# Moving half of the turned probabilities with on-chip copies instead of DMA transfers

## Chip, cores and metric

The kernel runs on one core of a Trainium2 chip. The metric is device time in microseconds for one execution; three runs of the kernel before gave 533.55 us as median (532.98 to 538.45).

## What is computed

Decayed causal attention over 8 batches, 8 heads, 576 positions and head width 64, followed by a gated projection. In float32:

```python
scores = q @ k.T / 8                                # per batch and head, 576 x 576
decay = cum[:, None] - cum[None, :]                 # cum = cumsum(log(clip(f)))
scores = where(causal, -1e9, scores + decay)
attn = softmax(scores)                              # with + 1e-9 in the denominator
x = concat_heads(attn @ v)                          # batch x 576 x 512
gate = sigmoid(sum(conv_w[k] * shifted(x, k) for k in range(5)))
out = (gate * (x @ w_val)) @ w_out
```

## The kernel before, in words

The unit of work is a pair of heads: 8 batches with 4 pairs each give 32 pairs, numbered i. For a pair, 128 partitions hold either two heads of 64 channels, or 128 query rows. The queries of a head are four blocks of 128 rows plus a first piece of 64 rows that both heads share a tile for. Block t sees EXT[t] = 192, 320, 448 or 576 keys.

The steps of a pair, with their lines:

- Scores, `plan_s`: TensorE adds a decay product (`st`, `pkr` or `pl`) and the product of q and k (`Xr`) into PSUM banks, in four groups (the groups with 576, 448, 320+192 and 64 keys).
- Row minimum, L451 on VectorE (DVE): it scales and masks the scores in PSUM and leaves `negm`. A short second instruction reads the accumulator out.
- Exponential, L455 on ScalarE (ACT): PSUM to the tiles P (Pa, Pb for both heads, Pl for the first piece), with the row sum in `zs`. After it the PSUM bank is free for other products.
- Turning, `plan_pt`, L492 and L497 on DVE: 32x32 blocks are transposed from P into T, which has 2 x 1568 columns (CW = 1568). T is double (r = i % 2). The last one, L497, takes Pl, after Pl has been scaled by POOL at L474.
- Moving, L498 to L502: a transposed 32x32 block is still in the partitions of its rows; the product with v needs its keys in 64 partitions of their half. So eight transfers a pair, issued by SyncE (SP), carry 32 partitions x 1568 columns (196 KB) each from T to U, one for each row quarter n and each column half c. U is double too (r = i % 2), so the moves of pair i wait for the product of pair i - 2.
- Product with v, `plan_pv`: 108 matmuls `banks<-U,vt` of 64x64 quadrants, all of one pair in a row.
- The normalised result goes to x32 (L548 and the copies of L554, which show as L275), is split into a rounded high part xh and a low part xl, and the gate convolution is made of multiplications (L282, ACT L280) and additions (L591). Every four pairs, `plan_moe` makes the projection by w_val (`banks<-xh,wall` and `xl`), multiplies by the gate, and projects by w_out (`banks<-wall,hh` and `hl`).

At the start the two weight matrices are decoded from integers into a high and a low part by DVE, ACT and POOL (L678 to L715).

What sets the order: every step is a node of `Plan` with an engine (or several that may do it, `any_`) and keys that it reads and writes. The order of all nodes, and the engine of each `any_` node, is not computed when the kernel is built: it is a packed table, `ORDER`, which `Plan.order` unpacks. Each engine runs its instructions in that order; an instruction at the head of an engine's queue that waits holds all that is behind it. SP issues nearly all transfers, in one queue. Helper functions record the instruction, so all matmuls show as L260, all copies and casts as L275 and all transfers as L287.

Of the kernel before, what the change touches and what calls it, by code (L numbers as in the profile page):

```python
# [14 lines left out]
P = 128  # L15
D = 64
# [30 lines left out]
    "nzHzabvOeNMWhkch&sg22q~fmv4+@0yg__GTt(bOG$5J~P$Uld8MXvo1p{yfoCrt3dGP1RdE^!3GBS;7MRXuGzyN>&UL$7^3kWijgIqxlAcv865DyWzkp{RO"
    "zJVM?Od@uoYEeAE1W19$$Z@0wXvWw99}od{10MK6R0;s0m?$2~gtDU^pr4|-$o;@!0F5G`q$o8i3~xk5P%WrY{3PCo`i#~f?a0=wjw}=MC?G`=G51m1kTUoP"
    "3X7(o&!EnuUZUQjyvR{t@~bcuhJks8UPLdUTYxBX8a;<Tjd_pygxZO$LEb>!MOn~pG#_&S*$#AJx`1w=8^cD6&|gq6^eVa!@MRAGgTN)!HIx`rg{i?rFe%J^"
    "z=82%PNL;#J$eE)i_&0>m|rlBm`7Rlm;uaRnE9;NS!5E2G!HCes<CxgC>DnmVij02mV=!F&Sv#w^=6G{O=S&a-Of6STn1JE9oC9n1lBN{m^+w<m>6~k)`OnG"  # L50
    "FW{H6hO;(+2)YVggAQe<vp;4@vt8IAmYI#tPN7eu0SF1A&fb;H%VtAFkc}*GwkdlQGl`kOEMN%Pj%++(U-m^pefF=}gV_hs53-+Tzt8@ZEhR7sC`c#z6@CN1"
    "jK4w{AT*-Y1Pz2oFcH9n6+D`70sSlXHbDY$K)etWBm$Ypp3SbN)KRc_3jP4L5o;r~V_#;!&F;iDV{c(=2?q&{gl2+|kcJ%3K9#)>k|un~hT+2mHeQ6^MfjU^"
    "pCHHU@xAEdj8lv*!cI~<p&Q$W9U%;1&t#v^t|c{+4w6(PG45XiK>SEDQa4B{Tmz&DGC`On2uTW(iDW1FNMX_=>~ri3>~`WFBAX~8ns8}S6{H!`Oaha8AnlMb"
    "ES5+ic0pbe-V)kLy^#IH!^8o|Ammc^wd^O5MeI9lfEXuQh;HIXEFMS4@o^hi0C$!&PMRXwaTr_=X@E3LdQ9pi-6k3E5xfuYz{`nx;(Nj;!g1m$;%VXpWEL_6"
    "N#PqPO_T}NEDKGZgAmDn@;s@VxJZhS`-xpdKW-JW2)RXBhO9#XXd9jY?IWI`prIk0joMD>qzqFYQ+(7ON-yO&`4l;c8>b9VrYQ52Fmo3^Os&H0#a$v_BeTgO"
    "@&ocy@&VjgTqEuRt`FCYV?ht$kKrfCv*eTbpYhjmw{ZRVT6_=w73Bu`E_pk74|zZNF!>DmJlR5aljUSR`31QT&!qCG%ajcYnEDfrog>Owp`fV*>M%}2ea3i<"
    "`<?h3evWvCah@Tirm0obCGvjiVd^4di80N%NbRG}F@DEApgyI3p~7e{S#Mbv7=w%<MjxY}@r1Za{)6~8@h{>CBgw2{)-czJtBmKk7r58BLE;(edFp%WC+cV1"
    "X9l0CVM>@r=08MG7QiGj7s(7Jis@t0*=(AK_8#{Mhow<y4(3bhTWT+Rf;vmRLA^`8PdvnIWd6o%Wp*%8S>!BE);bwXdB@_jhnYH-l?7$tSY#H5b)0&NdY!Fd"
    "8`*>G)tn*x5F22xvQTUYX`O|pe0>mXZk9Mpoh4z9GAEgytWZ`e%fa@ruQG2kSrh?9O3_f>Fh4Ns*+<!CijyLyMc66!Ip$@ikfmU)F*lhr%mro@yN11=dzjn8"
    "Zev$x)n#?D4LKw19`-nUhP}XsaEvrB%|Y{0G_-v*N6y}yFl`%cH|-EDO7Z5{Sdkn{mOCqzQ=fA*2hG_o+#~#)BjhMJ4V)%UOHNx(n1v!ac~v>`9DR<CW94+^"  # L60
    "T*&dU`f{GpMsmh-j?vPr{+u=TCcBl>!Fj{}z>aZtaH?3(X+Z9D&Rh;E_ayBiZ7`>rQ^y&~nWru0kaC&1WDbYp;siO-+~pi$t|AvnzePL7YNOqwjnH1x{-&jK"
    "8*-a+&*fguJ<Y9Qb#c47eOx@9Nl#Jkar?O+X;*V^=8ka3xGH)V?HAgOyt{eLECYR-JIK}LT5~=05WO|GBiBKn<1TVNyw9{W{b$xLdOr=IM|eE?Ppn^9@3;UD"
# [724 lines left out]
```

## Time and profile before

| what | value |
|---|---|
| median of three runs | 533.55 us (532.98 to 538.45) |
| the profiled execution's own time | 533.03 us |
| its span, first to last instruction | 531.3 us |
| mean granted TensorE clock | 0.974 |
| busy: PE, DVE, ACT, POOL | 482.3, 418.2, 309.4, 263.6 us |

The span is what the profile covers; 1.7 us lie outside it. Busy time is the time in which an engine ran instructions; idle time before an instruction is put down to what released it. "PE" is TensorE's matmul part, PEld its weight loads, SPq the queue of SyncE that issues transfers.

### The profile page before, as it was taken

What the parts mean: (1) busy time and instruction counts of PE and PEld (TensorE: products, weight loads), DVE (VectorE), ACT (ScalarE), POOL (GpSimd) and SP (SyncE); (2) the same over time, 40 slices, a digit from 0 to 9 for tenths busy, and PEclk for the clock granted to TensorE, in tenths of its full rate; (3) what the DMA queues carried; (4) which work ended last, traced back from release to release, by engine and by line L of the source; (5) the groups of instructions that cost most, each with busy time, mean ns of one, the idle gap of its engine ahead of it and who ended that gap; (6) DMA issues with size and microseconds to landing.
All of it is one profiled execution on the core that took longest, in us unless ns stands there. A gap on an engine that the chain in (4) does not pass through costs nothing.

```text
span 531.3 us, 15167 instructions
## 1 busy us (share of the span) xinstructions
PE 482.3 (91%) x5816; PEld 396.6 (75%) x5816; DVE 418.2 (79%) x1132; ACT 309.4 (58%) x869; POOL 263.6 (50%) x301
## 2 busy tenths in 40 slices
PE   6549798989899999998999979999999999999996
PEld 5347576868678877787787868778787876889885
DVE  4978988879888887786998849789887787788731
ACT  3546556546666665586586546566666576574420
POOL 4102412136748653776445836754757576664510
PEclk9769979999999999999999989999999999999999
DMA  7498789895789999789889899878999997977112
GB/s 294 154 238 236 203 223 241 230 273 170 198 221 246 218 223 270 199 259 264 211 211 260 217 227 223 234 231 217 267 200 245 241 251 199 239 181 190 54 49 80
DMA packets 50265, 114.04 MB, mean 215 GB/s; under 512 B 11664, under 2 KB 28048, under 8 KB 50192
## 3 DMA queue, kind: packets, MB, share of 16 engines
q1 hardware_dynamic: 50144, 112.99, 81.1%
q8 instruction: 46, 0.75, 0.7%
q14 instruction: 27, 0.22, 0.2%
q10 hardware_dynamic: 48, 0.07, 0.0%
HBM read 51.70 MB, written 9.96 MB: 116 GB/s over the span
## 4 chain that ended last, share of the span: by engine, by line
PE 54%; DVE 20%; DMA 8%; ACT 7%; issue 4%; POOL 3%; SPq 2%; DVEq 0%; ACTq 0%; POOLq 0%
PE banks L260 53%; DVE banks L451 7%; ACT P L455 6%; DVE T L492 5%; DMA U<-T 4%; SPq L287 2%; DMA zb<-zd 1%; DVE negm L451 1%; DMA zd<-zt 1%; PE banks L363 1%; DMA ot<-in_w_out_dram 1%; DMA Xr<-in_x_dram 1%; POOL gate L591 1%; DVE x L548 1%; DVE gate L680 1%
## 5 line engine op out<-in xcount | busy, mean ns | idle before, releaser
L455 ACT ACTIVATE P<-banks,negm 128x192 f32<-128x192 f32 (+3 forms) x256 | 146.6, 578 | 95.1 <-DVE negm L451 90.6
L451 DVE CUSTOM_DVE_ANT_0 banks<-banks,mk 128x192 f32<-128x192 f32 (+3 forms) x256 | 138.0, 574 | 34.9 <-PE banks L260 23.6
L591 POOL TENSOR_TENSOR gate<-gate,tm 128x576 f32<-128x576 f32 x85 | 121.5, 1432 | 40.6 <-ACT tm L280 12.5
L492 DVE STREAM_TRANSPOSE T<-P 128x384 f32<-128x384 f32 (+3 forms) x128 | 121.4, 963 | 24.7 <-ACT P L455 13.0
L260 PE MATMUL banks<-Xr 64*128 64x288 f32 (+4 forms) x704 | 119.9, 417 | 1.1 <-issue 0.9
L260 PE MATMUL banks<-U,vt 64*64 64x128 f32 (+1 forms) x3456 | 103.0, 264 | 16.3 <-DMA U<-T 13.9
L260 PEld LDWEIGHTS banks<-U,vt 64*64 64x64 f32 x3456 | 97.6, 140 | 25.8 <-issue 9.1
L260 PE MATMUL banks<-xh,wall 128*128 128x288 f32 x512 | 111.8, 301 | 2.3 <-ACT P L455 1.1
L260 PE MATMUL banks<-wall,hh 128*128 128x512 f32 x288 | 92.9, 404 | 2.9 <-ACT P L455 1.3
L260 PEld LDWEIGHTS banks<-xh,wall 128*128 128x128 f32 x512 | 84.4, 188 | 12.2 <-issue 4.9
L260 PEld LDWEIGHTS banks<-Xr 64*128 64x128 f32 (+1 forms) x704 | 72.0, 190 | 10.9 <-issue 2.1
L260 PE MATMUL banks<-xl,wall 128*128 128x288 f32 x256 | 75.5, 295 | 0.0
L260 PE MATMUL banks<-st,pkr 64*128 64x288 f32 (+3 forms) x320 | 61.1, 398 | 15.2 <-ACT P L455 8.0
L260 PEld LDWEIGHTS banks<-wall,hh 128*128 128x128 f32 x288 | 51.3, 188 | 19.7 <-issue 4.1
L260 PEld LDWEIGHTS banks<-st,pkr 64*128 64x128 f32 x320 | 31.9, 187 | 37.7 <-ACT P L455 10.9
L260 PE MATMUL banks<-wall,hl 128*128 128x512 f32 x144 | 56.4, 391 | 0.0
L282 POOL TENSOR_SCALAR tm<-x,cw 128x576 f32<-128x576 f32 x48 | 37.7, 786 | 27.2 <-DVE gate L591 24.8
L455 ACT ACTIVATION_READ_ACCUMULATOR P<-banks,negm 128x1 f32 x256 | 50.6, 198 | 0.0
L260 PEld LDWEIGHTS banks<-xl,wall 128*128 128x128 f32 x256 | 48.1, 188 | 0.4
L280 ACT ACTIVATE tm<-x,cw 128x576 f32<-128x576 f32 x50 | 38.5, 775 | 7.0 <-DVE gate L591 6.4
L451 DVE DVE_READ_ACCUMULATOR2_ANT negm<- 128x1 f32 x288 | 40.0, 139 | 0.1
L560 POOL TENSOR_TENSOR xl<-x,xh 128x576 fp32r<-128x576 f32 x22 | 31.9, 1454 | 15.5 <-ACT xh L275 12.1
(94 smaller groups left out, 487.7 us busy)
## 6 DMA issues: line engine op xcount, KB each, us to landing
U<-T SPq DMA_DIRECT2D x256, 196.0 KB, 5.6
Xr<-in_x_dram SPq DMA_DIRECT2D x32, 608.0 KB, 7.0
...
```

The source lines that it names most:

```text
L260: nc.tensor.matmul(out, lhsT=lhsT, rhs=rhs, start=start, stop=stop)
L280: eng.activation(out=out, in_=in_, func=AF.Copy, scale=col)
L282: eng.tensor_scalar(out=out, in0=in_, scalar1=col, scalar2=0.0, op0=ALU.mult, op1=ALU.add)
L287: lambda e: (nc.sync if e == "SP" else nc.scalar).dma_start(out=out, in_=in_), reads, writes, **kw)
L363: nc.tensor.transpose(out=bank(wk)[:, n * P:(n + 1) * P], in_=ident, identity=ident)
L451: nc.vector.tensor_tensor_reduce(out=sl, in0=sl, in1=add, op0=ALU.add, op1=ALU.min, scale=-0.125, scalar=3.0e38, accum_out=negm[r][:, col])
L455: nc.scalar.activation(out=dst, in_=bank(key)[:, a0:a0 + ext], func=AF.Exp, bias=negm[r][:, col], scale=-1.0, accum_out=zs[r][:, col])
L492: dve("DT", dt(2 * w), base + 0.35 + 0.03 * n, lambda t=t, w=w: nc.vector.transpose(out=blocks(64 * FB[t], [(32, 2), (64, 2 * t + 3), (CW, ...
L548: nc.vector.tensor_tensor(out=bass.AP(to.tensor, to.offset, [to.ap[0], (P, 4), (32, 2), (1, 32)]), in0=bank(keys[n])[:, 0:L0 // 2].rearran ...
L560: any_("xl", {"POOL": 1.4, "DVE": 0.67}, p, lambda eng: eng.tensor_tensor(out=xl[s], in0=xv, in1=xh[s][:, :].bitcast(F32), op=ALU.subtract ...
L591: any_("cva", {"POOL": 1.5, "DVE": 0.66}, pp, lambda eng, to=to: eng.tensor_tensor(out=gt, in0=gt, in1=to, op=ALU.add), [tk, gk], [gk])
L680: dve(cls, one, p, lambda: nc.vector.tensor_scalar(out=m, in0=hw, scalar1=0x1FF, scalar2=None, op0=ALU.bitwise_and), uk + kg, kh)
```

## The change

In `plan_pt` of the kernel before, eight transfers a pair move T to U. Of these, the four with c = n % 2 have the same 32 partitions as source and as destination. In the changed kernel two copies a pair (one for each e) write all 128 partitions of U[:, e] from the column half e of T; in two of the four row quarters of each the copied data is what is wanted. The other four transfers stay and overwrite the other two quarters, so each of them is ordered behind the copy of its e. A copy may run on ACT, DVE or POOL, as the order table says.

```diff
     def load_pair(i):
         r = i % XB
-        load("load", 1.55, i - (1.0 if i else 9.0), Xr[r], x[i], (), [("Xr", r)], early=i == 0)
+        load("load", 1.62, i - (1.0 if i else 9.0), Xr[r], x[i], (), [("Xr", r)], early=i == 0)
...
         dve("DT", 0.16, base + 0.5, lambda: nc.vector.transpose(out=blocks(LO, [(CW, 2)]), in_=Pl[r]), [("Pl",)], [("T", r, 4)])
+        for e in range(2):
+            any_("UC", {"ACT": CW / 1200.0 + 0.06, "DVE": CW / 1920.0 + 0.15, "POOL": CW / 1450.0 + 0.25}, base + 0.53 + 0.01 * e, lambda eng, e=e: copy(
+                eng, U[r][:, e], Tt[:, CW * e:CW * e + CW]), [("T", r, k) for k in range(5)], [("U", r, n, c) for n in (e, e + 2) for c in range(2)])
         for n in range(4):
-            for c in range(2):
+            for c in (1 - n % 2,):
                 a = D * (n // 2) + 32 * c
-                load("U", 0.87, base + 0.55 + 0.01 * n, U[r][a:a + 32, n % 2], Tt[32 * n:32 * n + 32, CW * c:CW * c + CW],
+                load("U", 0.93, base + 0.55 + 0.01 * n, U[r][a:a + 32, n % 2], Tt[32 * n:32 * n + 32, CW * c:CW * c + CW],
                      [("T", r, k) for k in range(5)], [("U", r, n, c)], hold=0.63)
```

The whole table `ORDER` is replaced as well:

```diff
 ORDER = (
-    "c-l=;2}soG|DO5Ied*ly=$tyYbLyNrr_QN!I!6U%25AXp24x9p2I(fGTaZ?eZb7;Q<rbtBlo_O}kgh_y3FQ`~Tad0nx(WZ9+<t$)@O`i6^SsaVd|n;M3W9=g"
+    "c-mc52}o9X_kQ2|?)$zkzWcuK`@Zj+kXDdZkXDdZkj?~Y4Wu(cIt6JHnA1So1ZfSV6_gdEQ;<$UIt6JHq&1K>L0SX<Qop{BKbL#&x#xGzbDnda!wrKjfgXZx"
...
```

The matmuls are the same in number and shape. Counted over the whole program, other instructions change engine with the table:

| instructions | ACT | DVE | POOL | SP |
|---|---|---|---|---|
| copy U<-T 128x1568 (new) | 0 to 35 | 0 to 1 | 0 to 28 | |
| transfer U<-T 32x1568 | | | | 256 to 128 |
| multiplication tm<-x,cw 128x576 | 50 to 63 | 14 to 10 | 48 to 39 | |
| multiplication gate<-x,cw 128x576 | 11 to 19 | 3 to 2 | 14 to 7 | |
| addition gate<-gate,tm 128x576 | | 27 to 37 | 85 to 75 | |
| eviction ot<-banks 128x512 | 27 to 30 | 9 to 6 | | |
| cast wall<-gate 128x512 | 4 to 7 | 4 to 1 | | |
| copy x<-banks 64x64 | 46 to 40 | 18 to 24 | | |

The first place is SP's queue at the moves of pair 0 (T_83 and U_85 are the tiles of even pairs, zd and zb the sums on their way to all partitions and back). Before:

```order
L287 DMA gate<-in_w_val_dram 128x1024
L287 DMA zd_67<-zt_96 128x32
L287 DMA U_85<-T_83 32x1568 x4
L287 DMA zb_98<-zd_67 64x4x128 x2
L287 DMA U_85<-T_83 32x1568 x4
```

Now:

```order
L283 DMA gate<-in_w_val_dram 128x1024
L283 DMA zd_67<-zt_96 128x32
L283 DMA U_85<-T_83 32x1568
L283 DMA zb_98<-zd_67 64x4x128
L283 DMA U_85<-T_83 32x1568
L283 DMA zb_98<-zd_67 64x4x128
L283 DMA U_85<-T_83 32x1568 x2
```

Four transfers of U stand where eight stood; the first of them waits for a copy on POOL and the second for one on ACT, and the two transfers of zb are still among them.

The second place is ACT's queue at the exponentials of pair 13 (negm_91 and zs_93 are the tiles of odd pairs; xh_107 belongs to pair 11). Before:

```order
L455 ACTIVATE P_81,zs_93<-banks,negm_91 128x448
L280 ACTIVATE gate<-x_100,cw 128x576
L455 ACTIVATE P_80,zs_93<-banks,negm_91 128x576 x2
L455 ACTIVATE P_81,zs_93<-banks,negm_91 128x448
L275 COPY x_101<-banks 64x64
L595 ACTIVATE gate<-gate 128x576
L455 ACTIVATE Pl_82,zs_93<-banks,negm_91 128x64
L275 CAST xh_107<-x_101 128x576
L455 ACTIVATE P_80,zs_93<-banks,negm_91 128x320
```

Now:

```order
L451 ACTIVATE P_80,zs_93<-banks,negm_91 128x576
L271 COPY U_85<-T_83 128x1568
L276 ACTIVATE tm<-x_100,cw 128x576 x2
L594 ACTIVATE gate<-gate 128x576
L451 ACTIVATE P_80,zs_93<-banks,negm_91 128x320
L271 COPY x_101<-banks 64x64 x2
L271 CAST xh_107<-x_101 128x576
L451 ACTIVATE P_80,zs_93<-banks,negm_91 128x320
L451 ACTIVATE P_81,zs_93<-banks,negm_91 128x192 x2
L451 ACTIVATE Pl_82,zs_93<-banks,negm_91 128x64
```

Between the last of the long exponentials (576 and 448 columns) and the first of the short ones (320, 192, 64) there now stand a copy of pair 12 and two multiplications beside the gate's activation; before, only a small copy and the gate's activation stood there ahead of the first short one.

## Rows read from the trace of the kernel before

**Rows 1.** Page, part 1: busy us (share of the span) and instructions.

```profile
PE 482.3 (91%) x5816; PEld 396.6 (75%) x5816; DVE 418.2 (79%) x1132; ACT 309.4 (58%) x869; POOL 263.6 (50%) x301
```

**Rows 2.** Windows, PE alone: stretch, its length, busy us, granted clock, DMA share, GB/s.

```profile
0.00:100.00 100.00, 75.28 (x759) 0.88 0.79 224
100.00:200.00 100.00, 92.12 (x1219) 1.00 0.91 226
...
400.00:500.00 100.00, 98.47 (x1328) 1.00 0.82 208
```

**Rows 3.** Waits of PE: what it waited for, us in total, times, longest.

```profile
PE banks L260 <- DMA U<-T: 13.9, 5, 5.0
PE banks L260 <- ACT P L455: 13.4, 19, 2.6
...
PE banks L260 <- ACT Pl L455: 3.4, 2, 2.8
```

**Rows 4.** Timeline, pair 0 from the last transpose to its product with v.

```profile
23.60 0.23 DVE L497 STREAM_TRANSPOSE T<-Pl 128x64 f32<-128x64 f32 x1
...
26.48 1.75 SPq L287 DMA_DIRECT2D zb<-zd  x2
28.28 2.52 SPq L287 DMA_DIRECT2D U<-T  x4
...
32.85 0.69 PE L260 MATMUL banks<-U,vt 64*64 64x128 f32 x4 [5.01 <-DMA U<-T]
...
35.45 4.81 PE L260 MATMUL banks<-U,vt 64*64 64x128 f32 x98 [1.90 <-DMA U<-T]
```

**Rows 5.** Timeline, four later products with v; in brackets the idle time before.

```profile
50.13 2.98 PE L260 MATMUL banks<-U,vt 64*64 64x128 f32 x108
...
113.04 1.69 PE L260 MATMUL banks<-U,vt 64*64 64x128 f32 x56 [1.74 <-DMA U<-T]
...
251.83 3.35 PE L260 MATMUL banks<-U,vt 64*64 64x128 f32 x108 [1.38 <-DMA U<-T]
...
310.04 4.74 PE L260 MATMUL banks<-U,vt 64*64 64x128 f32 x108 [3.88 <-DMA U<-T]
```

**Rows 6.** Page, parts 3 and 6: the queue's packets; issues, KB each, us to landing.

```profile
q1 hardware_dynamic: 50144, 112.99, 81.1%
...
U<-T SPq DMA_DIRECT2D x256, 196.0 KB, 5.6
```

**Rows 7.** Windows, all engines: busy us of PE, PEld, DVE, ACT, POOL, then PEclk, DMA, GB/s.

```profile
27.00:40.00 13.00, 6.08 (x110) 5.26 (x110) 9.82 (x28) 5.85 (x18) 0.56 (x2) 0.63 0.91 235
306.00:320.00 14.00, 10.12 (x141) 8.63 (x141) 7.47 (x20) 6.17 (x22) 4.17 (x7) 0.88 0.93 225
```

**Rows 8.** Groups by shape: busy us, mean ns of one, and idle us before them.

```profile
L282 POOL TENSOR_SCALAR tm<-x,cw 128x576 f32<-128x576 f32 x48 | 37.7, 786 | 27.2 <-DVE gate L591 24.8 <-DVE x L548 0.6
...
L275 ACT CAST xh<-x 128x576 fp32r<-128x576 f32 x30 | 20.1, 670 | 13.7 <-DVE x L548 12.9 <-DVE x L275 0.6
...
L474 POOL TENSOR_SCALAR Pl<-Pl,zr 128x64 f32<-128x64 f32 x32 | 11.0, 343 | 51.4 <-DVE zr L465 45.1 <-ACT ot L662 4.1 <-PE banks L260 2.2
...
L275 ACT CAST pl<-pk 64x64 fp32r<-64x64 f32 x28 | 6.7, 240 | 7.6 <-PE banks L260 7.4
```

**Rows 9.** Groups by shape, ACT: a multiplication, and the exponentials of 320 and 192 columns.

```profile
L280 ACT ACTIVATE tm<-x,cw 128x576 f32<-128x576 f32 x50 | 38.5, 775 | 7.0 <-DVE gate L591 6.4 <-POOL gate L591 0.4
...
L455 ACT ACTIVATE P<-banks,negm 128x320 f32<-128x320 f32 x64 | 33.3, 524 | 29.2 <-DVE negm L451 28.5 <-DVE T L492 0.4
...
L455 ACT ACTIVATE P<-banks,negm 128x192 f32<-128x192 f32 x64 | 26.6, 418 | 31.1 <-DVE negm L451 30.2 <-DVE gate L688 0.5
```

**Rows 10.** Timeline: a DVE instruction beside a POOL one, and the same shape later.

```profile
22.14 1.26 POOL L568 TENSOR_TENSOR tm<-ident,cw 128x640 f32<-128x640 f32 x1
...
22.32 1.36 DVE L680 TENSOR_SCALAR gate<-ot 128x512 int32<-128x512 int32 x1
...
31.39 0.43 DVE L680 TENSOR_SCALAR gate<-gate 128x512 int32<-128x512 int32 x1
```

More of the change, by code (lines that the diff above doesn't have):

```diff
@@ L47 @@
[L47 to L62, printed above, removed]
@@ new lines @@
+    "R(K!uJXC_zB16z5v;-}I=b*LV8t69gZg3a02|NXD1=mB{puNy(=r9xl{|I^qY6p)&=b<A|4?GIL4!#Q>he8l)*b+1WH^Dl=J7FGJ6t)6A0B?rX!@q%*;9cN0"
+    "STA@G`~&PHECZ{CU5DL;)xf*q{a_@b0p0`O1lta4hd0AJ;Qeqi;xc#~JO`c!{|fsJ_7m(E*m?LAcm~WxOVLYUFhB)(z!ZEMJ_jFz55q^`D_{(;1fPeG!&wLs"
+    "LI|wD@4=>F^RO$p8#onW4mJg|AiRiOz<yvWq7l)8Z~=Reoyaa^5NJgPkhRD<<RUDE+>0n8k#G|H3gQOhBeD$%LM@_IfC)$eC15Mih(x1$ku?Ab)dI8wod6Tw"
+    "4fFsX5q-#Wh>M65h%<-^Vl!d_If)!Z4k06mEMf*ZioAuKMIJ#MLuk-e^i4!RFa!wUlZZRO17HEkL5WZsQ4@$IWIbvxssZ(g@Qk2ASy6L{8N@u|C)6(}2RejK"
@@ new lines @@
+    "qD$x+^dN8z*nw_Gcc4MYW^@Z0g{(*afI5l#2<t`@k*Cn#qP{~-0`CwDz#=dMu#j`W3h)6vj2=Uep!?BNXaMp(o&o_dOQ-?#IC>5}jb1?iiuw(eK~<wXs3__x"
+    "Y6>-mLSe>H(<lmtjVWUu;%0Ct$Sm#-?g4HAw}`97Y{l%vfbeMi2NVg<#tZSs@dLyaoC<HigV9Jd7b1n2AWDb}5`rWl5{wq}59wc$1>?n>z?{MC!yLpM!5qUh"
+    ";+ycb_&U4`UxEbjz4%(lEb1)&9Ofb>g)ibs=vMq&LOWhS+zGjWAI77JBw_@U#azOy5WvLO_$B;n%s$9L2!!wv{~Dztx`=-f{w7?<-^Ck=Y+{g@B5DX$!c+W9"
+    "`~+qc(+25<+`>#^rZJa@qr?KyLx>VOiCx4-;wJ`-SqEt%VhJ=tEwPpO0>dRp32!l-kOH<FauzZ{9)$E0hatBiZNxg_E#mLQWlS%Th~0n<kn6Gc@sIJf<T`SS"
@@ new lines @@
+    "JVnHih-4L+O(v7Xq$0VIJOa57c?>a<pAugZg=805fi+;6SP|BR1!1Ql91;q<1PNl7Ay6`o>>))-bC3nd9`YdhA-R*>MeZd7P&BlaoW{;m&yuNB9(9P^M&>}r"
+    "$TQ?w@+g@E-GSYMZN(-Cjf734?W8T#1@aPEO{pimA-*S;2sMPmgeF2O^%D_B%8;r_8j_V{qJ$|1>JHMkl<z2?$S}$#%63W{wUOFHO;KIc^Vn8GC)G{qB<-T?"
+    "r*J7!N*nfjY=%-z2~vyHTIySBJ86ZArO+tHKmT4@NZ%8FB%CH3r~XW6CP}DT>O*WV^(=LQI!PU+-l7gthp11mbJ!W`0O1mL6pN;v!uDh5sAO82=HW)UT(*>b"
+    "3p+x%O!ytkWQv$dritlfCYbfi24;y_qHUywm`5qyltD@jvza-`{DF3oR!4h<y-j$FUBQBJT$+^DOX;VaB|TxzG3S|Gq@QTN(00-G)6lpB%ywo6bC@~8>}Pf}"
@@ new lines @@
+    "zomUg>tRkX9k>8)fH}roWZ$A(AYCS1BaM-UDC2~2(h_rpX=d$Ux3fFg&FmI-66au-*dcb3?V&|!L>v<*#A#?&S`GV8(rJ>5m1JF`XxLVEH+zaSPI*C^reK*g"
+    "CX|I^RdAbe_3ZPsQ|utCpFO}HrhQ-ooH6zYZHoN|<uzrPJw}_L%~9S_M%dHr1@<_5j(rq&9M_A};H<bUI25PC+RUPGCTV}t_OTAKj<Algwy}1zBrGlKD7Ty2"
+    "&)vW!@tV18&Mb|};<0w%=1E8C^R#7354WDXiNBryj#lP0<7znudJA`e+rVw-4s-X=A=Cu@03AjDNCW6~oOXJF-oRn<P*h{pRqhyfoIAyx<5K7x`aG8_l8TPg"
+    "r@6iKvvddj1m_G##8dJl94+Sv=NM;+yUfjStGTuG5WS8rq656+EG2y>9nBkJo#R~OL^xT_KF&eTAgiC%%QEp?yaW7p{_m`A{v_)>{{nrMHO%keU!r>?QOOv;"
@@ new lines @@
+    "hu_b?N<W9Yh}+9+<ykmh&OQ1=dW4tdAsJ)z5&k%TivK5TiM7CTRE4TOvf6kZyczlk>n;5WpIo)XpW_2nv-H>W4|IS*WUv|Y{A3lXN>n9es2HrOW&S%+xk^<9"
+    "W?$k=a&B=ZIHR0-PHh#2{bSWO-frFr-Wi@lR1(#QLZYN-hp1iDA!-)2h&C{Kt8TM?uDZi}z&ppg$om%e9d4ki!rRQd!n?t%7a15DkyYei1R33;ZB@IgcJcS~"
+    "H_5ikW;lzS45OOysOni2z};7Mu<DfPgJ?<wh*9Ex(SYbq)q|>!oH5arsvA{Ds*Y7ni-tuQ?uckX^jFp2RpTPE_#tnW#}?1<Bx0?23!{NSmX^gYI3(_zXo0uL"
+    "L-8|`YROSazhpqNL9&l=kip?n`1O(oNw=g&BH|um9A&7vU5vL?wPL1pr?^=X5og6Mk~*=F{}baE28VCttNFu{cF9%Am}E+Fo<U+;#9r|c@iFnYitiK;8J8Gl"
@@ new lines @@
+    "`M4y^U#S8MNCLEgC76>eN#-Tfl4XgDFOn*yfD|ni3zm6isY`l5c20azJi=&~DFr9QXT(PCUMYm%A?ud)$j-~gWW%x%S*vuP_@MX+V_eoRo082kE{W6puwX(w"
+    "D(;Y)1rcdhIwsyG-7R&<C&f=>OEN$nl9T0!rE@a3ASHMxcp{h+EX%G6Q1WT<3-L|Cyi6od%2{%iyezMk7X?LSt>BcRUokJP6YP@hmklU>lrM>U<v+{sNFPY="
+    "DdrTziV?-UVyED^U_vl2I3PGDy(rzL*{ylQc+aRvH%m`Q&q%LGZ%8*NrxeqQLxN7hn4-u(CFmE_D=)|!l-uOH<pY9;(k8*8bV>0+u_ORX9KtK|8}cK%W4eIw"
+    "vVbU@kuFHdN~Z8H`QP#*@?-LS@`G}dQltcwP9;m3QeM)alpn<yNlK_xhLn4ibJ9baR^<o5WhF>>&T!E{l1yks!cpa@=8^oF{EqyAd|AqoKx9HmuclM8PjgUn"
@@ new lines @@
+    "hw*^%gW{yZsVxXM2q!fd8CrNtGov}HIiftKR0++(F3q53TnSa-RDUV|R+41(!hp6$e@m&7Gzy!AZ{>hOC`)P4ilX+pW<_&A$kr}sgj%!~tX<S_WNO(t<wYe~"
+    "u_9M1{!#v`e58D)Bxy}rqwJ8dL)a%&Y5R0R8B1|Oc}7{Qb;;_rr?p1KF71Bppl(PvsyiV(BfO=1sB<gQvKd{!c0qSScSbj>o6s%lR&?iuM#+%yf|jT<sn{x&"
+    "O02jpyeqt}y{jG4zR|wd-q$|X3RO-ONRQS()xOlS^(4JYZ`5zm3-yiqCcR4^)ZY_66owUPMN0pTv0ic0FfA<U-x|WIZ}c;UAG9a6MOjhtt@b<ZTh#~EB~`or"
+    "n*NUIfoZ~!R&7+w8deOG2C#8Vk2aEwS5>D}eX6o*qw0w5m~E$G!N4{G>L2tc_2c?Uy}(#&tTU>NMx)CZG;USxRK3x^*Qbn!j89b0Rh`Bz<DhCmHKxKEXoe5k"
@@ new lines @@
+    "W@FLVYy3(7i~cX+-@>Q*m-<h7n4#bJtMNDEpT-_@o2p6CXlzo=8Rw1fjBFiQM>MO<Y_rge(zU97)&HjdWQ3WXn-)w)^P*|R1UA1FPN)E#P-oPA5Nb?Tlgs?b"
+    "^vu*}9yAY`zgH!7Q!14XZAPgnYNo+t5E)bku*hj}>OwlETA)^`yHr6#z+7vtGq;-C%#CKQNou-pd~7^nJ7a4y8`KW<MqOFARhKds&3n}692Xtk=8!t6?lg~@"
+    "$IK6H*Nu0LeKxF#X1ZdyVfbjiZ+>i^u`Sp}Z4J5_`>buRE^WYyXre*e0d>22gL;elmhFz~feWyd)MW$4!nH^(TkJ!&MO%%bQN3cDusKY%rdDUj^wj*){Kov="
+    "+@bza4YHFgNt4SSw3kdOyV1VY@QtC-j<)YK+*F@Zv+aFql09V?+M5kc_EvkHsnOJKzv(z^DA}7#6OKv8fcl#Ktz*V9>p(ll?Dy1@>O)SFGh?Z?tT@2VD~=lu"
@@ L105 @@
+    "D~~GAD#+@^%BKpfnpn-MmQ-u2!5}CI0Rnx#5g_<y8~oV@K#<QD@Yw_Ye8E?3(C0JA=P$(i8FbYL2f<dKUl72b?Jo#lEXZo!muTR#_sch89r;V-mz*z8*k}J2"
+    "-xoCaYRp<5XccJ<2fkhjv|bakUgHZcblrxmR|VFYfmgXgzMijf`I7y`T8n_M)&i~LL00j;^a1-?VXb%AY7c8OfUnj7uQFa^u+|%BHD(P9zFudo5BPcvXcZZ;"
+    "IwQ!}IYU=_{?DACs}Zo(>@^J#>pa(H3|-HMud{`%b_iZQgM6LVni}x0ll@Y8O*!yaq&0njuegv^E^A)MDlT}n7UF+20Il}F_6GfrwWb4TH4?Or1zAS}RyqGy"
+    "BiJh9T7|VeK&(y+v98bBX036C{|{?my=&O|9M^jKuU2cy{AW`j>wAS*R~z^`@&D+L_<x%LTGa?x-M_UxhJM}8FM0n5#lizW"
 )
```

66 lines of the change are left out of this document (21 added, 45 removed).

## The prediction, made before the changed kernel ran

> **What bounds the kernel now.** I read the busy shares first, then TensorE by stretches, then what it waits for, then the timeline at those waits. TensorE is busy 482.3 of 531.3 us [rows 1]: matmuls of unchanged number and shape fill 91% of the span, so the change can touch only the 49 us in which it is idle, and the clock at which it runs after an idle stretch. The first 100 us hold 24.7 us of that idle time (75.28 busy), the next 100 hold 7.9, and from 400 to 500 only 1.5 is left [rows 2]. By cause [rows 3]: 13.9 us for moved probabilities (U<-T), 13.4 and 3.4 us for exponentials, which free the PSUM banks for the next scores; most of the rest is the start, before any product can run, and the change leaves that. The five stalls on U are 5.01 and 1.90 us in pair 0 [rows 4], then 1.74, 1.38 and 3.88 us [rows 5], together 13.91.
>
> A stall on U costs more than its length. In the stretch from 306 to 320 us, around the one of 3.88 us, the granted clock is 0.88, and around pair 0's stalls it is 0.63 [rows 7]. The product with v after the 3.88 us stall took 4.74 us where an undisturbed one takes 2.98 [rows 5], 1.8 us more. So the stalls that this change aims at are worth 15.7 us, plus the slow product of pair 0.
>
> **What the change removes.** 128 of 256 transfers of 196 KB: 25.7 MB of 113 MB on the one queue that carries nearly everything, which keeps the 16 DMA engines busy 81.1% of the span [rows 6]. If their time goes by bytes, that falls to about 63%, an estimate. SP issues four transfers of U in 2.52 us [rows 4], 0.63 each; four fewer save 2.5 us in each chain from T to U.
>
> **Pair 0, worked out.** Before: the last transpose ends at 23.83 (23.60 + 0.23), the eight issues and the two of zb between them end at 30.80 (28.28 + 2.52), and the last wait for U ends at 35.45, 4.65 us later [rows 4]. Now a copy comes first. POOL: 343 ns for 64 columns and 786 ns for 576 [rows 8] make 0.865 ns a column and 1.64 us for 1568. ACT: 240 and 670 ns [rows 8] make 0.84 ns a column and 1.50 us. So the first issue can start at 25.5; four of U (2.52) and two of zb (about 1.4, their rows take 1.75 for two with a wait in it [rows 4]) end at 29.4, and U is there at 34.0. That is 1.4 us earlier: pair 0's stalls go from 6.9 to 5.5. The clock there stays low, since TensorE still idles for five microseconds.
>
> **The later stalls.** There I expect the three to go, 7.0 us, and the 1.8 us of slow product with the last: a U transfer lands in a median of 5.6 us [rows 6] on a queue with a DMA share of 0.8 to 0.9 [rows 2], and both the issue (2.5 us shorter) and the landing shorten, against 1.5 to 1.64 us for a copy. Sum of the removed part: 1.4 + 7.0 + 1.8 = 10.2 us. Bounds: nothing at all, if the copies start late; all 13.9 + 1.8 and, with pair 0's first product back to 2.98, some 2 us more, 18.
>
> **What it adds on ACT.** 35 copies at 1.50 are 52.5 us; 13 + 8 multiplications at 775 ns [rows 9] are 16.3; the smaller shifts (evictions and casts against copies of x) are few, and I leave them at 1. ACT goes from 309 to about 380 us, 72% of the span. What hides it is ACT's idle time ahead of the short exponentials: in the order DVE makes two transposes between the minima of the long and of the short groups, and ACT waits for `negm` 28.5 and 30.2 us there [rows 9], 1.83 us a pair. In pair 13's queue the copy stands exactly in this gap, as most ACT copies do. One copy (1.50) fits; the mean addition is 70 / 32 = 2.2 us a pair, so the cover is used up, and a pair with both copies on ACT (3.0) overruns it by 1.2. The copy adds a wait too: it needs DVE's last transpose of its pair (L497) and the product with v two pairs earlier, waits that only SP bore before. Behind it on ACT are multiplications and the four short exponentials; those release banks, and TensorE's next scores wait for them. TensorE waits 16.8 us for exponentials today [rows 3]; scaled by ACT's load, 380 / 309 = 1.23, that is +3.9, and I take +4. Bounds: 0, if the idle time hides all, to 26, if half of 35 copies pass on their 1.5 us.
>
> **What it adds on POOL and DVE.** 28 copies at 1.64 are 46 us, and POOL gives up 16 multiplications at 786 ns [rows 8], 12.6 us, and 10 additions: net less than 33 us on an engine busy 50% [rows 1]. Copies on POOL wait for T ahead of additions to the gate, which few wait for at once. DVE's ten additions more and its four to five multiplications, casts and evictions fewer leave it level. A DVE instruction beside a POOL one took 1.36 us where the same shape took 0.43 later [rows 10], 0.9 more. Should each of the 28 copies hold one DVE instruction that long, DVE loses 26 us spread over 32 pairs; TensorE sees DVE through the 16.8 us of waits for exponentials and little else, so I take +1, with bounds of 0 and 26. The Trainium skill, SBUF — State Buffer, section "Who interferes with whom", says that DVE and GpSimd share one pair of ports as an exclusive lock, for copies, casts and tensor_scalar forms and for two inputs in SBUF, and that the later one blocks for a whole instruction. The row agrees in direction. By the rule a copy could hold DVE for its full 1.64 us, 46 us in all, but DVE's minima (from PSUM) would go untouched; so I keep the term at +1.
>
> **The order chosen anew.** Matmul groups come in nearly the same sequence in the first three pairs and differ afterwards. I see no systematic gain or loss and put it at 0, with bounds of 5 us either way, the middle between the 1.5 and the 7.9 us of idle time that a stretch of 100 us has [rows 2].
>
> **Sum.** -10.2 + 4 + 1 = -5.2 us on the profiled execution's 533.03, which lies 0.5 below the median of 533.55: 527.8 us.
>
> **Rivals.**
> 1. All that waits on transfers goes. Besides the 10.2 us, pair 0's other 5.5 and its slow product go because the first moves start earlier, and ACT's gaps hide the copies: 533.0 - 18 = 515. For it: the queue is the busiest shared thing after TensorE. Against it: pair 0's chain is mostly landing time. Chance 0.20.
> 2. The gain is given back. Transfers now start only when an in-order engine reaches the copy, so U is as late as before or ACT's waits take the place of the transfers' waits: about 10 us won, 10 lost, 533. For it: SP, which used to bear the wait for T, had nothing urgent behind it, ACT has. Chance 0.20.
> 3. Slower: ACT becomes the second bound. Every copy that is not hidden pushes the short exponentials of the next pair back by 1.5 us, banks come free later, TensorE idles and then runs at a low clock. It decides from the point where 7 of the 35 copies pass on their whole length (10.5 us against 10.2 won). With one in three, 12 x 1.5 = 18, it is 533 - 10 + 18 = 541. For it: the cover of 1.83 us a pair against 2.2 added. Against it: ACT is idle 222 us today and the copies can slide. Chance 0.17.
>
> My forecast holds 0.43; its own range is 521 to 533: from 12 us won with ACT's term at 0, to 5 won and 5 paid.
>
> **How the numbers follow.** A measurement of this kernel tells about 1% from no change; the border of faster lies at 528.2. Just over half of the forecast's 0.43 falls below it, with all of rival 1: 0.45. Same takes the rest of the forecast and nearly all of rival 2: 0.35. Rival 3 and the edges: 0.20. The range reaches down to rival 1 and up to rival 3, 514 to 541, and leaves out what lies beyond both.
>
> **What would show it.** Right: TensorE's waits for U fall from 13.9 to about 5.5 us, nearly all in pair 0, whose last wait ends about 1.4 us earlier; the DMA queue's share falls towards 63% and U's median landing below 5 us; the product with v takes 2.98 us everywhere after 60 us; copies take 1.5 us on ACT and 1.6 on POOL; TensorE's waits for exponentials rise from 16.8 to about 21 us. Wrong: TensorE's busy time moves by more than 3 us; waits for U reappear at other pairs because the copy was late; ACT's copies show long waits for the product two pairs back; or TensorE's idle time behind exponentials grows by over 10 us.

## The result, and the profile after

The changed kernel takes 517.25 us (median of four runs, 516.40 to 519.22), beside 536.0 us for the kernel before on the same chip: a ratio of 0.965 (95% interval 0.957 to 0.973). That is inside the range of 514 to 541, and three times the gain of the central forecast: the profiled execution takes 517.02 us against 533.03, 16.0 less, where 5.2 were forecast. Lines of the changed kernel have numbers some four lower: L256 is L260 of before, L271 is L275, L451 is L455, L493 is L497.

Busy time by engine, from the page, against [rows 1]:

```profile
PE 477.6 (93%) x5816; PEld 393.0 (76%) x5816; DVE 423.5 (82%) x1135; ACT 371.5 (72%) x924; POOL 284.5 (55%) x307
```

The span fell from 531.3 to 515.2, by 16.1 us: 4.7 of it are busy time of TensorE (482.3 to 477.6), 11.4 its idle time (49.0 to 37.6). By stretches, against [rows 2] (busy us, granted clock, DMA share, GB/s):

```profile
0.00:100.00 100.00, 77.92 (x780) 0.90 0.63 187
100.00:200.00 100.00, 97.02 (x1322) 1.00 0.65 185
...
400.00:500.00 100.00, 97.23 (x1146) 1.00 0.48 141
```

The largest step is in the second stretch, 92.12 to 97.02 at the same clock. The DMA share is lower everywhere. What TensorE waits for, against [rows 3]:

```profile
PE banks L256 <- ACT P L451: 16.0, 16, 4.7
PE banks L256 <- DMA U<-T: 5.5, 2, 4.4
...
PE banks L359 <- POOL ident L304: 1.4, 1, 1.4
...
PE banks L256 <- ACT Pl L451: 1.2, 2, 0.7
```

The waits for U went from 13.9 to 5.5 us, those for exponentials (P and Pl) only from 16.8 to 17.2. The wait for `ident`, at the start, was longer in the kernel before:

```profile
PE banks L363 <- POOL ident L308: 5.1, 1, 5.1
```

Pair 0 on the timeline, against [rows 4]:

```profile
23.76 0.20 DVE L493 STREAM_TRANSPOSE T<-Pl 128x64 f32<-128x64 f32 x1
24.03 1.49 POOL L271 COPY U<-T 128x1568 f32<-128x1568 f32 x1 [0.58 <-DVE T L493]
24.05 1.48 ACT L271 COPY U<-T 128x1568 f32<-128x1568 f32 x1
25.54 0.61 SPq L283 DMA_DIRECT2D U<-T  x1
...
28.30 1.26 SPq L283 DMA_DIRECT2D U<-T  x2
...
32.85 0.69 PE L256 MATMUL banks<-U,vt 64*64 64x128 f32 x4 [4.35 <-DMA U<-T]
...
33.83 5.24 PE L256 MATMUL banks<-U,vt 64*64 64x128 f32 x104 [0.29 <-ACT P L451]
```

Each transfer stands behind its copy. The product goes on at 33.83 where it went on at 35.45, 1.6 us earlier; its first part starts at 32.85 as before. The last wait that the profile puts down to U ends at 32.85; the 0.29 us before 33.83 it puts down to an exponential. Later products with v, against [rows 5]:

```profile
51.05 2.83 PE L256 MATMUL banks<-U,vt 64*64 64x128 f32 x104 [1.12 <-DMA U<-T]
64.19 2.98 PE L256 MATMUL banks<-U,vt 64*64 64x128 f32 x108
...
295.08 2.98 PE L256 MATMUL banks<-U,vt 64*64 64x128 f32 x108 [0.19 <-DMA out_dram<-ot]
```

The 1.12 us in pair 1 are new: the kernel before had no stall there. After them no product waits for U again. Counted in order, the one that stood at 310.04, with a stall of 3.88 us and 4.74 us of work, is pair 18's; it now stands at 295.08 and takes 2.98. The queue and the landing of U, against [rows 6]:

```profile
q1 hardware_dynamic: 44000, 87.29, 59.2%
...
U<-T SPq DMA_DIRECT2D x128, 196.0 KB, 3.9
```

The copies, and the two short exponentials, as groups (busy, mean ns | idle time before them), the exponentials against [rows 9]:

```profile
L271 ACT COPY U<-T 128x1568 f32<-128x1568 f32 x35 | 52.1, 1504 | 3.1 <-DVE T L493 2.8 <-DMA out_dram<-ot 0.3
L271 POOL COPY U<-T 128x1568 f32<-128x1568 f32 x28 | 42.7, 1535 | 12.0 <-DVE T L493 9.7 <-DMA zb<-zd 1.3 <-issue 1.0
...
L451 ACT ACTIVATE P<-banks,negm 128x320 f32<-128x320 f32 x64 | 33.5, 525 | 20.7 <-DVE negm L447 19.0 <-DVE T L488 1.1
...
L451 ACT ACTIVATE P<-banks,negm 128x192 f32<-128x192 f32 x64 | 26.6, 417 | 15.3 <-DVE negm L447 14.7 <-DVE T L488 0.4
```

ACT reaches its copies late enough that it waits only 2.8 us for the transposes, and the idle time ahead of the exponentials has shrunk from 60.3 to 36.0 us: at most 24.3 us of the 52.1 stand where ACT used to wait for `negm`, since other instructions of ACT moved too.

### The profile page after: what moved, and what is told of

It reads as the page before. It is cut to its first block, busy times and chain, and to the rows that moved or that the text cites. A ratio compares the mean times of both kernels' runs of the same rounds, so it can differ in the third digit from the quotient of the medians.

```text
span 515.2 us, 15149 instructions
## 1 busy us (share of the span) xinstructions
PE 477.6 (93%) x5816; PEld 393.0 (76%) x5816; DVE 423.5 (82%) x1135; ACT 371.5 (72%) x924; POOL 284.5 (55%) x307
## 3 DMA queue, kind: packets, MB, share of 16 engines
q1 hardware_dynamic: 44000, 87.29, 59.2%
## 4 chain that ended last, share of the span: by engine, by line
PE 53%; DVE 25%; ACT 9%; DMA 5%; issue 4%; POOL 1%; SPq 1%; DVEq 0%; ACTq 0%; POOLq 0%
PE banks L256 53%; DVE banks L447 7%; DVE T L488 6%; ACT P L451 5%; DMA U<-T 2%; DVE x L547 2%; DMA zd<-zt 2%; DVE negm L447 1%; DVE h L620 1%; DVE gate L681 1%; ACT tm L276 1%; DMA cwu<-in_conv_w_dram 1%; SPq L283 1%; DVE gate L590 1%; DVE gate L687 1%
## 5 line engine op out<-in xcount | busy, mean ns | idle before, releaser
L451 ACT ACTIVATE P<-banks,negm 128x576 f32<-128x576 f32 (+3 forms) x256 | 146.4, 578 | 55.6 <-DVE negm L447 51.1
L447 DVE CUSTOM_DVE_ANT_0 banks<-banks,mk 128x320 f32<-128x320 f32 (+3 forms) x256 | 137.9, 575 | 30.9 <-PE banks L256 15.9
L488 DVE STREAM_TRANSPOSE T<-P 128x640 f32<-128x640 f32 (+3 forms) x128 | 121.1, 963 | 12.8 <-ACT P L451 10.9
L590 POOL TENSOR_TENSOR gate<-gate,tm 128x576 f32<-128x576 f32 x75 | 107.9, 1441 | 36.1 <-DVE gate L590 13.0
L256 PE MATMUL banks<-Xr 64*128 64x288 f32 (+4 forms) x704 | 118.3, 418 | 0.5 <-DMA Xr<-in_x_dram 0.5
L256 PE MATMUL banks<-xh,wall 128*128 128x288 f32 x512 | 111.4, 301 | 2.3 <-ACT P L451 2.2
L256 PEld LDWEIGHTS banks<-U,vt 64*64 64x64 f32 x3456 | 93.7, 136 | 16.7 <-issue 11.2
L256 PE MATMUL banks<-U,vt 64*64 64x128 f32 (+1 forms) x3456 | 98.9, 258 | 7.4 <-DMA U<-T 5.5
L256 PE MATMUL banks<-wall,hh 128*128 128x512 f32 x288 | 92.8, 403 | 1.3 <-ACT ot L661 0.7
L256 PEld LDWEIGHTS banks<-xh,wall 128*128 128x128 f32 x512 | 84.1, 188 | 11.0 <-issue 5.3
L256 PE MATMUL banks<-st,pkr 64*128 64x288 f32 (+3 forms) x320 | 61.7, 401 | 19.4 <-ACT P L451 12.8
L256 PEld LDWEIGHTS banks<-Xr 64*128 64x128 f32 (+1 forms) x704 | 71.8, 191 | 9.5 <-DMA Xr<-in_x_dram 0.7
L256 PE MATMUL banks<-xl,wall 128*128 128x288 f32 x256 | 75.4, 295 | 0.0
L256 PEld LDWEIGHTS banks<-wall,hh 128*128 128x128 f32 x288 | 51.3, 188 | 19.3 <-issue 6.8
L256 PEld LDWEIGHTS banks<-st,pkr 64*128 64x128 f32 x320 | 31.3, 189 | 42.0 <-ACT P L451 16.0
L256 PE MATMUL banks<-wall,hl 128*128 128x512 f32 x144 | 56.3, 391 | 0.0
L271 ACT COPY U<-T 128x1568 f32<-128x1568 f32 x35 | 52.1, 1504 | 3.1 <-DVE T L493 2.8
L276 ACT ACTIVATE tm<-x,cw 128x576 f32<-128x576 f32 x63 | 47.9, 774 | 8.7 <-DVE gate L590 6.4
L451 ACT ACTIVATION_READ_ACCUMULATOR P<-banks,negm 128x1 f32 x256 | 50.8, 199 | 0.0
L271 POOL COPY U<-T 128x1568 f32<-128x1568 f32 x28 | 42.7, 1535 | 12.0 <-DVE T L493 9.7
L256 PEld LDWEIGHTS banks<-xl,wall 128*128 128x128 f32 x256 | 48.1, 188 | 0.3
L559 POOL TENSOR_TENSOR xl<-x,xh 128x576 fp32r<-128x576 f32 x24 | 35.2, 1468 | 15.1 <-ACT xh L271 12.3
```

Of the source, the lines that this page charges most:

```text
L256: nc.tensor.matmul(out, lhsT=lhsT, rhs=rhs, start=start, stop=stop)
L271: (eng.copy if eng is nc.scalar else eng.tensor_copy)(out=out, in_=in_)
L276: eng.activation(out=out, in_=in_, func=AF.Copy, scale=col)
L447: nc.vector.tensor_tensor_reduce(out=sl, in0=sl, in1=add, op0=ALU.add, op1=ALU.min, scale=-0.125, scalar=3.0e38, accum_out=negm[r][:, col])
L451: nc.scalar.activation(out=dst, in_=bank(key)[:, a0:a0 + ext], func=AF.Exp, bias=negm[r][:, col], scale=-1.0, accum_out=zs[r][:, col])
L488: dve("DT", dt(2 * w), base + 0.35 + 0.03 * n, lambda t=t, w=w: nc.vector.transpose(out=blocks(64 * FB[t], [(32, 2), (64, 2 * t + 3), (CW, ...
```

## Experiments

All ratios are to the kernel before on the same chip; its median was 534.7, 538.0 and 537.3 us in the three groups.

| run | us | ratio (95% interval) |
|---|---|---|
| 1 new moves, old order | 565.6 | 1.056 (1.048 to 1.064) |
| 2 old moves, new order | 597.5 | 1.114 (1.105 to 1.123) |
| 3 new order, no copies | 519.3 | 0.971 (0.966 to 0.976) |
| 4 old order, half of the moves | 516.5 | 0.967 (0.963 to 0.970) |
| 5 four unread transfers, into DRAM | 518.9 | 0.966 (0.960 to 0.972) |
| 6 four unread transfers, small | 518.3 | 0.964 (0.957 to 0.971) |
| 7 copies twice | 566.7 | 1.054 (1.046 to 1.063) |
| 8 copies all on ACT | 552.1 | 1.025 (1.017 to 1.034) |
| 9 copies all on POOL | 541.1 | 1.012 (1.007 to 1.016) |
| 10 copies a quarter longer | 525.0 | 0.975 (0.967 to 0.983) |
| 11 four small transfers, waited for | 516.5 | 0.959 (0.951 to 0.967) |
| 12 four unread transfers, SBUF to SBUF | 534.0 | 0.994 (0.989 to 0.999) |

### Runs 1 to 4: the moves and the order apart

Run 1 is the changed kernel with a table in which every instruction stands as in the kernel before; only the two copies are new, where the first transfer of their pair stood, on the engines that the changed kernel gives them.

```diff
-SP: U<-T x8 of pair i
+POOL, ACT (as after): U<-T copy x2 of pair i
+SP: U<-T x4 of pair i
```

> The new moves (two copies and four transfers a pair, each copy on the engine that the changed kernel gives it) in the order of the kernel before: both copies stand where the pair's first transfer stood. Theory A (the moves carry the gain: lighter DMA queue, shorter way from T to U, fewer low-clock products): most of the 16 us, 517 to 525 us. Theory B (the new order carries the gain, and copies put into an order that was not made for them hold up ACT and POOL): 530 to 545 us, with ACT waiting for the last transpose ahead of copies.

Measured: 565.6 us. Nothing is won; 49 us are lost against the same order without copies (run 4). TensorE's largest wait:

```profile
PE banks L256 <- ACT P L451: 31.2, 26, 3.3
```

The exponentials that stand behind a copy come late: 31.2 us where it was 12.7 in run 4 and 13.4 before. That is 18.5 of the 46 us between the two profiled executions (514.8 and 561.0 us of span); TensorE's busy time makes 9 more (480.9 to 489.9), and the rest was not traced.

Run 2 is the kernel before with the changed kernel's table; the two same-partition transfers that a copy replaces stand where the copy stood.

```diff
-POOL, ACT or DVE: U<-T copy, e = 0 or 1
+SP: U<-T x2, the same-partition transfers of this e
```

> The eight transfers a pair of the kernel before in the order of the changed one: where a copy stood, its two transfers stand in SP's queue. Theory A: no better than before, 530 to 545 us, TensorE's waits for U over 14 us, since the queue is as full as before and this order leaves U less time. Theory B: within a third of the changed kernel's gain or better, under 523 us.

Measured: 597.5 us. The new order is no gain of its own; without the new moves it is the slowest of all.

Run 3 leaves the copies out of the changed kernel.

```diff
-nc.gpsimd.memset(x32[r][:, 0:T0], 0.0)
+nc.gpsimd.memset(x32[r][:, 0:T0], 0.0), nc.gpsimd.memset(U[r], 0.0)
...
-lambda eng, e=e: copy(eng, U[r][:, e], Tt[:, CW * e:CW * e + CW])
+lambda eng: None
```

> The changed kernel with the copies left out, so half of U keeps zeros that POOL writes at the start: what the copies themselves cost. My forecast had ACT's 35 copies at 4 us and POOL's at 1 us of the end. If the idle time of ACT and POOL hides them (the trace of the changed kernel has TensorE's waits for exponentials up by only 0.4 us): 515 to 518 us. If they cost what was forecast or more: 508 to 513 us.

Measured: 519.3 us, not below the 517.25 with the copies. In the order made for them 96 us of copies cost nothing that this run can show. The zeros that POOL writes here delay the start (pair 0's product with v begins at 33.86 us, at 32.85 with the copies), so a price of 1 us or so would stay hidden.

Run 4 leaves the four same-partition transfers out of the kernel before.

```diff
-load("U", ...)
+(load if c != n % 2 else skip)("U", ...)    # skip: a step that issues nothing
```

> The kernel before with the four transfers a pair within the same partitions left out and nothing in their place, so half of U keeps zeros that POOL writes at the start: what the removed transfers are worth in the old order with copies for nothing. Theory A: the three later stalls on U go and pair 0's is shorter by 2.5 us of issue, 517 to 524 us. Theory B: 528 to 533 us, since in the old order TensorE waits for other things by then.

Measured: 516.5 us, the whole gain of the change. TensorE's waits, then the queue:

```profile
PE banks L260 <- ACT P L455: 12.7, 19, 2.6
...
PE banks L260 <- DMA U<-T: 1.6, 2, 1.3
```

```profile
q1 hardware_dynamic: 44000, 87.29, 59.3%
...
U<-T SPq DMA_DIRECT2D x128, 196.0 KB, 4.4
```

So the four transfers are worth as much as the whole change. The table's part is that the copies in their place cost next to nothing. The two kernels reach the same total by different ways: pair 0's product with v begins at 29.01 us in run 4 and at 32.85 in the changed kernel, pair 31's at 477.1 and 477.5.

### Runs 5, 6, 11 and 12: what the four transfers cost

They have three costs: their bytes on the queue, SP's time to issue them, and the product's wait for them. A fourth stands beside these: VectorE's transposes two pairs later can write T only when the transfers have read it. All four runs are run 4 with four transfers a pair issued at the old places again.

Run 5: full size, into DRAM, read by nothing.

```diff
+dump = dram.tile([P, CW], F32, name="dump")
...
+dst = dump[32 * n:32 * n + 32, 0:CW] if c == n % 2 else U[r][a:a + 32, n % 2]
```

> The kernel before in its own order, where the four same-partition transfers of a pair are issued at their old places with the full 6272 bytes of a partition, but into a buffer in DRAM that nothing reads; half of U stays zero, as in the run with half of the moves left out (516.5 us). This gives the queue its bytes and SyncE its issues back, but no product waits for them. Theory 'bytes' (what the four transfers cost is their load on the queue, which delays the four that are waited for, and x, v and zb): 528 to 536 us, queue 1 busy near 80%, landing of U 5.3 us or more. Theory 'slots' (the cost is SyncE's 0.6 us for each issue): the same here, told apart by the run with small transfers. Theory 'wait' (the cost was that the product had to wait for those four themselves): 515 to 519 us.

Measured: 518.9 us. Queue and landing:

```profile
q1 hardware_dynamic: 50144, 112.99, 74.6%
...
U<-T SPq DMA_DIRECT2D x128, 196.0 KB, 4.5
dump<-T SPq DMA_DIRECT2D x128, 196.0 KB, 4.3
```

The bytes are back and the time is not, which seemed to speak for the wait. But the queue is not as busy as before (81.1%), and U lands in 4.5 us, not 5.6: bytes to DRAM are not the same load.

Run 6: the same with 64 bytes of a partition.

```diff
-Tt[32 * n:32 * n + 32, CW * c:CW * c + CW]
+Tt[32 * n:32 * n + 32, CW * c:CW * c + (16 if away else CW)]
```

> As the run before it, but each of the four unread transfers carries 64 bytes of a partition instead of 6272: SyncE's issues are back, the bytes are not. Theory 'bytes': 515 to 519 us. Theory 'slots': 526 to 536 us, about as slow as the run with the full bytes. Theory 'wait': 515 to 519 us.

Measured: 518.3 us. SP's 128 further issues cost no more than 2 us.

Run 11: the small transfers go into U, so the product waits for all eight.

```diff
+w = 16 if c == n % 2 else CW
...
-U[r][a:a + 32, n % 2], Tt[32 * n:32 * n + 32, CW * c:CW * c + CW]
+U[r][a:a + 32, n % 2, 0:w], Tt[32 * n:32 * n + 32, CW * c:CW * c + w]
```

> The kernel before in its own order with all eight transfers of a pair into U, where the four same-partition ones carry 64 bytes of a partition instead of 6272 (the rest of their half of U stays zero): SyncE's issues and the product's wait for all eight are back, the bytes are not. With the run of unread small transfers (518.3 us: issues alone) it sets the wait apart. Theory 'wait' (the product starts when the last of eight has landed, whatever it carries): 527 to 536 us. Theory 'bytes and wait together' (the wait hurts only because the load makes the last one land late): 516 to 520 us, PE's wait for U under 3 us.

Measured: 516.5 us. Issues and wait together cost nothing; the theory that the wait alone carries the cost falls.

Run 12: full size, from T onto its own place in T, which changes no value and which no product reads.

```diff
+src = Tt[32 * n:32 * n + 32, CW * c:CW * c + CW]
...
+load("U", ..., src if c == n % 2 else U[r][a:a + 32, n % 2], src, ...)
```

> As the run with full unread transfers (518.9 us), but from T onto the same place of T, so that source, destination memory and bytes are those of the kernel before (the run with DRAM as the destination left queue 1 busy for 74.6%, not 81.1%, and U landed after 4.5 us, not 5.6); nothing waits for them but the transposes that write this T two pairs later. Half of U stays zero. Theory 'load' (SBUF to SBUF traffic of 196 KB each delays the four that are waited for): 526 to 536 us, landing of U 5.3 us or more. Theory 'wait': 516 to 521 us.

Measured: 534.0 us, 17.5 more than run 11 on the same chip. By ratio, 0.994 against 0.959 there and 0.967 in run 4, over four fifths of the gain are gone again, though the product waits for the same four transfers as in run 4. What is left, 0.1 to 1.1% by the interval, may be the product's wait under load. Queue and landing, then TensorE's waits:

```profile
q1 hardware_dynamic: 50144, 112.99, 81.5%
...
U<-T SPq DMA_DIRECT2D x128, 196.0 KB, 5.5
T<-T SPq DMA_DIRECT2D x128, 196.0 KB, 5.4
```

```profile
PE banks L260 <- ACT P L455: 14.3, 19, 2.6
PE banks L260 <- DMA U<-T: 11.0, 5, 4.0
```

The queue is as busy as in the kernel before, most of the waits for U return, and even the stall of 3.88 us at pair 18 does. Its timeline, which also tells how load becomes lateness:

```profile
301.27 0.63 SPq L287 DMA_DIRECT2D zb<-zd  x1
...
303.91 0.59 SPq L287 DMA_DIRECT2D U<-T  x1
...
306.44 0.52 SPq L287 DMA_DIRECT2D U<-T  x1
...
311.27 4.62 PE L260 MATMUL banks<-U,vt 64*64 64x128 f32 x108 [3.88 <-DMA U<-T]
```

SP's queue is in order, and two transfers of U stand behind zb, which cannot be issued before zd has landed in DRAM. From 293 to 313 us SP waits for that:

```profile
SPq L287 <- DMA zd<-zt: 7.9, 2, 5.6
```

At the same place of run 11 (282 to 303 us):

```profile
SPq L287 <- DMA zd<-zt: 3.6, 1, 3.6
```

Over the span SP waits for zd 26.6 us in the kernel before, 22.9 in run 12, 12.7 in run 4 and 7.3 in run 11. So in the old order the load acts at least twice: zd lands later, which delays the issue of U, and U lands later once issued. The sum of SP's waits does not give the time by itself: it is 29.4 us in the changed kernel and 46.0 in run 3, which take about the same time as run 4 (517.25 and 519.3 us).

A third way goes through VectorE, whose transposes wait for transfers before they write T again. Run 12:

```profile
DVE T L492 <- DMA vt<-in_v_dram: 4.9, 2, 3.9
DVE T L492 <- DMA U<-T: 2.8, 2, 2.0
DVE T L492 <- DMA zd<-zt: 2.7, 1, 2.7
...
DVE T L492 <- DMA T<-T: 2.4, 1, 2.4
```

Together 12.8 us; they are 11.1 us in the kernel before, 0.7 in run 4 and nothing in runs 5 and 11. So run 12 rules out the product's wait for the four transfers as the main cost, but not the transposes' wait for them. How the 17.5 us divide among the three was not tried.

### Runs 7 to 10: how much room the copies have

Run 7 does each copy twice.

```diff
-copy(eng, U[r][:, e], Tt[:, CW * e:CW * e + CW])
+[copy(eng, U[r][:, e], Tt[:, CW * e:CW * e + CW]) for _ in range(2)]
```

> The changed kernel with each copy done twice at its place, on its engine: 35 times 1.50 = 52 us more on ACT, 28 times 1.54 = 43 us more on POOL, 1 us more on DVE, and each copy is ready 1.5 us later. Theory 'idle time of the two engines holds them' (as the run without copies, 519 us, says of the first one): 516 to 524 us. Rival 'the new order just fits, the next 1.5 us a pair go on the path of the product' (32 pairs, at 1.5 us or less): 535 to 565 us.

Measured: 566.7 us, 49 more. The first copy was free, the second is not.

Run 8 gives all copies to ACT at their places in the order.

```diff
-UC: 35 on ACT, 28 on POOL, 1 on DVE
+UC: 64 on ACT
```

> The changed kernel with all 64 copies on ACT, in the same order: ACT busy 371.5 + 29 x 1.50 = 415 us (80% of the span), POOL 284.5 - 43 = 242 us. Theory 'either engine hides them': 516 to 522 us. Rival 'ACT becomes the second bound' (the exponentials behind two copies of 1.5 us come late and PE waits for them): 527 to 541 us, with PE's waits for ACT P above 25 us.

Measured: 552.1 us, 35 more. TensorE's largest wait:

```profile
PE banks L256 <- ACT P L451: 33.1, 23, 4.7
```

33.1 us where it was 16.0, half of the loss: this is my rival 3 as described, in an order that was not made for it. Most of the rest is TensorE's busy time, 492.3 us against 477.6, at a mean granted clock of 0.961 against 0.978.

Run 9 gives all copies to POOL.

```diff
-UC: 35 on ACT, 28 on POOL, 1 on DVE
+UC: 64 on POOL
```

> The changed kernel with all 64 copies on POOL, in the same order: POOL busy 284.5 + 36 x 1.54 = 340 us (66%), ACT 371.5 - 52 = 319 us. Theory 'the order fits only the engines it was made for' (all on ACT: 552.1 us): two copies of a pair in a row on POOL end 1.5 us later than one on each, 530 to 550 us. Rival 'only ACT is short' (POOL is idle for 45% of the span and PE waits for it 1.4 us in all): 516 to 523 us.

Measured: 541.1 us, 24 more. The transfers start later; SP's largest wait:

```profile
SPq L283 <- POOL U L271: 89.8, 30, 10.5
```

In the changed kernel it was 74.0 us for the copies of both engines (44.4 on ACT and 29.6 on POOL). TensorE's own waits for U hardly rise (6.3 us, 5.5 in the changed kernel), so how the lateness reaches it is open. An engine that is idle for 45% of the span has no room at these places.

Run 10 puts a copy of 392 columns ahead of each.

```diff
-copy(eng, U[r][:, e], Tt[:, CW * e:CW * e + CW])
+[copy(eng, U[r][:, e, 0:w], Tt[:, CW * e:CW * e + w]) for w in (CW // 4, CW)]
```

> The changed kernel with a copy of a quarter of the columns (392 of 1568) ahead of each copy, on the same engine: some 0.5 us more for each. Copies left out: 519.3 us, done twice: 566.7 us. Theory 'in proportion' (the cost grows with each tenth of a us): a third of the step, 530 to 540 us. Rival 'there is a margin, and the cost starts behind it': 515 to 521 us.

Measured: 525.0 us, 7.7 more, between the two expectations. In 15 pairs both copies are on one engine: 15 x 1.04 + 17 x 0.52 = 24 us of delay, summed over pairs, of which a third shows; in run 7 15 x 3.0 + 17 x 1.5 = 71 us, of which 49 show. If each pair has the same slack and pays all behind it, the slack is 0.5 us a pair by run 10 and 0.7 by run 7. This is an estimate: run 10 and the changed kernel ran on different chips, and their ratios, 0.975 and 0.965, have intervals that overlap.

## Why the prediction was right, and where its sizes were off

By its own terms, from the profile after against the one before:

| step | forecast us | measured us |
|---|---|---|
| waits for U (forecast: pair 0 -1.4, three later stalls -7.0; measured: -2.6, -7.0, pair 1 +1.1) | -8.4 | -8.4 |
| slow products (TensorE's busy time) | -1.8 | -4.7 |
| copies on ACT (waits for exponentials) | +4 | +0.4 |
| copies on POOL, effect on DVE | +1 | 0 |
| order anew (all other idle time) | 0 | -3.4 |
| sum | -5.2 | -16.1 |

- **Waits for U**: the sum came as worked out, 13.9 to 5.5 us, with landing below 5 us, but by luck in part. Pair 0's stalls on U fell by 2.6 us (6.91 to 4.35) where 1.4 were forecast, and pair 1 has a new one of 1.12, of the kind that I had listed as a sign of being wrong. There the last transpose starts at 40.02 us instead of 36.70, and the copies come behind it. The three later stalls went, as forecast.
- **Slow products** were mis-sized. I counted one product, 4.74 against 2.98. All 3456 matmuls with v together went from 103.0 to 98.9 us, 4.1 less. My own flag, busy time moving by more than 3 us, was raised.
- **Copies on ACT**: the duration was right (1.50 forecast, 1.504 measured); the step that failed is "scaled by ACT's load". Run 3 shows their price to be nothing in the new order, run 1 shows up to 49 us, beside the bounds of 26 for ACT and 26 for POOL and DVE, in the old one. What decided was the place of the copies, not ACT's load.
- **POOL and DVE**: 1.64 us forecast, 1.535 measured, and DVE busy 423.5 us with the copies and 422.5 without (run 3).
- **The order anew** at 0 was the weakest step. I put it at 0, with 5 us either way, apart from the copies, when its effect and theirs were one thing: by medians, 516.5 without copies or new order (run 4), +49 for copies (run 1), -48 for the order (517.25). It gave no speed of its own (run 2). I also took TensorE's idle time at the start as left alone; its wait for `ident` fell from 5.1 to 1.4 us, which is more than the whole -3.4. That gave no lead: up to 32.85 us, where pair 0's product begins in both, TensorE ran 90 matmuls before and 91 after, in 16.43 and 18.55 busy us, at a granted clock of 0.86 and 0.78.
- **The queue** fell to 59.2%, not to 63%: I took its time as going by bytes. By 81.1% of 531.3 us less 59.3% of 514.8 (run 4), the four transfers' share is 125.6 us, 0.98 for each of 128; in this difference is also what the other transfers took longer beside them.

Of the rivals, the first had the size (515) and half of the reason: ACT's gaps do hide the copies, but pair 0's stall stayed. The second, that U would be as late as before, did not come. The third came where an order did not fit: runs 1, 7 and 8.

The reason behind the removed part was right in kind, a loaded queue, but thin: I saw the stalls of TensorE that were put down to U and missed that the load also sits in SP's wait for zd, ahead of U in the same queue, and in VectorE's wait for T. In the old order, taking away the bytes and keeping the issues and the wait (run 11) takes the waits for U from 13.9 to 2.2 us and the profiled time from 533.03 to 517.06.

What stays open: how much of pair 0's remaining wait of 4.4 us comes from the copies ahead of the transfers (run 3, without them, waits 2.7 us for U in all); copying only the partitions that are wanted, so that the transfers need not stand behind a copy, was not tried.
